# Layer 1's second product with its operands' roles exchanged: weight words stationary, blocks of 512 tokens moving

## The chip, the cores and the metric

One core of a Trainium2 chip runs the whole kernel. The metric is the device time of one execution in microseconds. The kernel before took 1139.12 us, the median of three runs (1136.8 to 1140.69).

## The reference

Chunked attention, then two feed-forward layers on the same 3072 tokens (4 batches of 768), all in float32; the weights are given in float64 on input.

```python
B, H, S, D = 4, 8, 768, 64          # attention: chunks of 32, 16 left, 8 right, 8 memory keys
scores = scale * q_c @ k_full.T     # per chunk; k_full = memory keys + the chunk's window
out_c = softmax(scores) @ v_full
x = out.transpose(0, 2, 1, 3).reshape(3072, 512)
h = x @ w_in                        # layer 1: 512 -> 2048
g = h * tanh(softplus(h))           # Mish
x = g @ w_out                       # 2048 -> 512: "layer 1's second product"
h = x @ w2_in                       # layer 2: 512 -> 2048
g = h * sigmoid(1.702 * h)
out = g @ w2_out                    # 2048 -> 512
```

## The kernel before, in words

The work runs in four stages that overlap at their seams: attention with layer 1's first product (`quads`, `forward`), layer 1's second product (`second(1, k)`), layer 2's first product (`first`), layer 2's second product (`second(2, k)`). Every matmul operand but the earliest is a pair of words, high and low (float32r): a high part is a rounded copy (ScalarE, or VectorE), a low part a VectorE difference, and a product is three matmuls: high-high, high-low, low-high.

**Order.** Every operation is given to a planner (`Plan`, lines 85 to 227) with a rank, a cost and the buffers that it reads and writes. The planner runs a list schedule: on each engine the ready operation of least rank. The order it finds is fixed in each engine's queue, and all DMAs but the earliest are issued from SP's queue in that order. `T[name].new` takes the next of a tag's buffers; it waits until the operations of the buffer's last use are done. One unit of rank in the second products is one product of 24 matmuls.

**Layer 1's first product** (`forward`, line 1004). For each block of 384 tokens (8 of them) and each of 16 slices of 128 features, 12 matmuls of 384 columns go to one of four PSUM banks; ScalarE or VectorE copies the bank to a staging buffer (gh and gl in turn, three buffers each), and SP stores it in DRAM as g1d. Features are on partitions, tokens in rows.

**Layer 1's second product** (`second`, line 1225). One level of Strassen-Winograd: tokens fall into two halves (th), features into two (fh), and outputs into two of 256 columns; instead of eight block products there are seven, on operands that are sums and differences of blocks (`comb`). A call `second(1, k)` takes 128 tokens of each half. It loads four blocks a11, a12, a21, a22 of 128 x 1024 numbers (8 feature slices of 128 tokens each) from g1d, applies Mish, and combines them. In `step` each operand is split into gh and gl, and 24 matmuls (8 slices x 3) go to one bank: the activations' words are the stationary operand (128 features x 128 tokens), the weights' words the moving one (256 columns). So the sums have tokens on partitions. `row` then turns them with four TensorE transposes of 128x128 against the identity, copies the bank of 512 columns to a u buffer and stores that in x1d, where features are on partitions again. There are 12 calls of 7 products.

**Layer 2's first product** (`first`, line 1161). Also seven products, here with weights stationary and 384 columns of x moving; `x_prep` (line 1073) loads x1d, forms differences in the v buffers, and splits the seven operands into homes named in `places` (line 1042). The first three operands are prepared during calls 9 and 10 of the second product (line 1387), the other four at its end.

Buffers that the change touches: `ql`, `kl`, `qT`, `kT`, `mem_t`, `aT` (attention), `gh`, `gl`, `u` (three buffers each), `mask`; and `own`, the four tiles wi0 to wi3 that layer 1's first weights leave free.

Of the kernel before, what the change touches and what calls it, by code (L numbers as in the profile page):

```python
# [27 lines left out]
class Buf:  # L28


    def __init__(self, tag, shape, dtype):
        self.tag, self.shape, self.dtype = tag, shape, dtype
        self.tile = None
        self.gate = []
        self.closed = False
        self.writers, self.readers, self.users = [], [], []
        self.whole = self

# [3 lines left out]
    def get(self):  # L42
        if self.tile is None:
# [12 lines left out]
class Tag:  # L56
# [4 lines left out]
    def new(self, shape, dtype):  # L61
        b = Buf(self, shape, dtype)
        self.made.append(b)
        return b
# [20 lines left out]
class Plan:  # L85
# [10 lines left out]
    def add(self, rank, ways, reads=(), writes=(), updates=(), chain=None, table=None):  # L96
# [33 lines left out]
        for b in (*reads, *writes, *updates):  # L130
            assert not b.whole.closed
            b.whole.users.append(op)
        if chain is not None:
# [109 lines left out]
def kernel(  # L243
# [46 lines left out]
    def tags(pool, **bufs):  # L290
# [214 lines left out]
    mask = fixed(sb.tile([P, 3, P], F32, name="mask"))  # L505
# [498 lines left out]
    def forward(j, f):  # L1004
# [31 lines left out]
        load(i + 0.4, gds[key], [lambda: (g1d[s, 2 * th + fh][:, p, :], t.get())], P * TB * 4, 1536, [t])  # L1036

    K2 = KD // 2
# [4 lines left out]
        ("ql", "kl", "qT", "kT"), ("gh", "gh", "gl", "aT"), ("gh", "aT", "gl", "gl"),  # L1043
# [29 lines left out]
    def x_prep(s, wanted, kts, rank, gap=0.0, stage="st", at="vt"):  # L1073
# [7 lines left out]
        def half(kt, a, rank):  # L1081
            if stage == "u" and kt and a:
                ts = [T[stage].new([P, TB], F32) for _ in range(2)]
                for i, t in enumerate(ts):
                    c = (2 * s + i) * TB
                    load(rank - 3, t, [lambda t=t, c=c: (t.get(), x1d[:, a * K2 + kt, c:c + TB])],
                         P * TB * 4, 1536, [x1s[3 * s + i] for i in range(3)])
                return [(t, t.get) for t in ts]
            st = T["st" if stage == "u" else stage].new([P, 2, TB], F32)
            load(rank - 3, st, [lambda: (  # L1090
                st.get(),
                x1d[:, a * K2 + kt, 2 * TB * s:2 * TB * (s + 1)].rearrange("p (s t) -> p s t", s=2),
            )], P * TB * 8, 3072, [x1s[3 * s + i] for i in range(3)])
# [129 lines left out]
    turn2 = [0]  # L1223

    def second(layer, k):
# [3 lines left out]
        r = RB[layer] + 7 * k  # L1229
        ha, hc = (T[x].new([P, H2], F32) for x in banks[k % 2])  # L1230
        src = (g1d, gd)[layer - 1]

        def block(blk, tag, rank):
            t = T[tag].new([P, NP, P], F32)
            load(rank - 2, t, [lambda: (t.get(), src[s, blk][:, :, j * P:(j + 1) * P])],
                 P * NP * P * 4, 512, [gds[layer, s, blk, p] for p in range(NP)])
            if layer == 1:
                add(rank, [("act", act(NP * P), lambda: nc.scalar.activation(
                    out=flat(t), in_=flat(t), func=AF.Mish))], updates=[t], table="mish")
# [9 lines left out]
        def step(i, n, src, bank, fresh):  # L1249
# [11 lines left out]
            w = [wb[layer, p, kind] for p in range(NP)]  # L1261
# [13 lines left out]
            if i == 0:  # L1275
                kw["writes"].append(pace.setdefault((layer, k), fixed()))
            add(r + i, [("pe", 3 * NP * 0.1175, go)], reads=reads, **kw)

        def row(th, t):
            r0 = 2 * TB * s + th * TB + j * P  # L1280
            if layer == 2:
                load(r + 6.5, fixed(), [lambda: (out[r0:r0 + P, :], t.get())], P * DM * 4, 2048, [t])
                return
# [157 lines left out]
```

## Time and profile before

| | |
|---|---|
| median of 3 runs (lowest, highest) | 1139.12 us (1136.8, 1140.69) |
| the profiled execution | 1139.0 us, span 1137.0 us |
| TensorE matmul / weight load busy | 98% / 94% |
| VectorE / ScalarE busy | 74% / 56% |
| granted TensorE clock, mean | 0.993 |
| DMA | 217.94 MB, mean 192 GB/s |

Busy is the union of an engine's recorded instructions. Matmuls are pipelined and their recorded durations overlap, so the pace of the engine is read from one start to the next. A group's name is out<-moving,stationary for a matmul, out<-in for others, without buffer numbers: o, s, h are PSUM banks; wo, wi, vt, xh, xl, u are buffers in SBUF. PE is TensorE's matmuls, PEld its weight loads, DVE VectorE, ACT ScalarE, SPq the queue that issues DMAs.

### The profile page before, as it was taken

How to read it: one execution, taken by the hardware profiler on the slowest of the kernel's cores; microseconds unless marked ns; L12 is line 12 of the kernel's file. 1: busy time of each engine (PE TensorE's matmuls, PEld its weight loads, DVE VectorE, ACT ScalarE, POOL GpSimd, SP SyncE). 2: the span in 40 equal slices, each digit the busy share in tenths (PEclk: the TensorE clock that was granted, in tenths of full speed). 3: DMA queues.
4: the chain of work that ended last, by engine and by line, in shares of the span. 5: the costliest groups of instructions: out<-in, count | busy, mean ns of one | idle time of the engine just before them, and what ended most of it. 6: DMA issues, size and time to landing. Idle time of an engine off the chain costs nothing.

```text
span 1137.0 us, 22649 instructions
## 1 busy us (share of the span) xinstructions
PE 1117.1 (98%) x8320; PEld 1070.3 (94%) x8320; DVE 841.8 (74%) x1878; ACT 632.3 (56%) x1478; POOL 10.1 (1%) x29
## 2 busy tenths in 40 slices
PE   7899999999999999999999999999999999999998
PEld 6667999999999999999999999999999999999998
DVE  5898877887776668779787776847566877786875
ACT  4776566666566456675675566555566443333422
POOL 2000000000000000000000000000000000000000
PEclk8899999999999999999999999999999999999999
DMA  9975778768976856556564478777688644536351
GB/s 167 276 205 140 205 203 249 200 166 219 233 231 223 259 152 196 169 156 201 174 187 137 129 255 257 247 249 240 227 262 266 200 133 122 148 103 166 112 151 53
DMA packets 325741, 217.94 MB, mean 192 GB/s; under 512 B 136120, under 2 KB 300743, under 8 KB 325631
## 3 DMA queue, kind: packets, MB, share of 16 engines
q1 hardware_dynamic: 325279, 215.76, 65.7%
q8 instruction: 65, 1.06, 0.4%
q0 software_dynamic: 352, 0.75, 0.4%
q14 instruction: 45, 0.37, 0.1%
HBM read 135.18 MB, written 81.26 MB: 190 GB/s over the span
## 4 chain that ended last, share of the span: by engine, by line
PE 93%; DVE 3%; DMA 1%; SPq 1%; ACT 1%; issue 0%; DVEq 0%; ACTq 0%
PE o L1268 18%; PE h L1019 13%; PE o L1019 13%; PE h L1268 12%; PE s L1268 11%; PE h L1179 9%; PE o L1179 8%; PE s L1179 4%; PE o L712 1%; PE s L712 1%; PE s L929 1%; PE o L929 1%; PE s L908 1%; PE o L908 1%; SPq L306 1%; PE o L1288 1%
## 5 line engine op out<-in xcount | busy, mean ns | idle before, releaser
L779 ACT ACTIVATE e<-e,mx 96x128 f32<-96x128 f32 x240 | 93.0, 394 | 4.8 <-DVE mx L764 4.8
L1268 PE MATMUL o<-wo,xh 128*128 128x256 f32 x456 | 85.8, 284 | 0.0
L1258 DVE TENSOR_TENSOR xl<-wi,xh 128x1024 fp32r<-128x1024 f32 x64 | 77.7, 1222 | 8.3 <-ACT xh L1255 7.4
L1019 PE MATMUL h<-xh,wi 128*128 128x384 f32 x320 | 83.8, 343 | 0.0
L1019 PE MATMUL o<-xh,wi 128*128 128x384 f32 x320 | 83.5, 342 | 0.0
L1258 DVE TENSOR_TENSOR xl<-vt,xh 128x1024 fp32r<-128x1024 f32 x48 | 58.3, 1222 | 20.1 <-ACT xh L1255 19.3
L1268 PEld LDWEIGHTS o<-wo,xh 128*128 128x128 f32 x456 | 70.6, 190 | 0.0
L1255 ACT ACTIVATE xh<-wi 128x1024 fp32r<-128x1024 f32 x50 | 52.6, 1054 | 23.1 <-PE h L1268 9.7
L1268 PE MATMUL o<-wo,xl 128*128 128x256 f32 x228 | 64.4, 283 | 0.0
L1268 PE MATMUL o<-wi,xh 128*128 128x256 f32 x312 | 58.7, 282 | 0.0
L1268 PE MATMUL s<-wo,xh 128*128 128x256 f32 x312 | 58.5, 283 | 0.0
L1019 PEld LDWEIGHTS h<-xh,wi 128*128 128x128 f32 x320 | 56.7, 188 | 1.7
L1019 PEld LDWEIGHTS o<-xh,wi 128*128 128x128 f32 x320 | 56.8, 188 | 1.3
L1019 PE MATMUL o<-xl,wi 128*128 128x384 f32 x160 | 53.8, 337 | 0.0
L1019 PE MATMUL h<-xl,wi 128*128 128x384 f32 x160 | 53.8, 336 | 0.0
L1149 ACT ACTIVATE e<-h 128x384 f32<-128x384 f32 (+1 forms) x53 | 23.5, 444 | 48.4 <-PE h L1268 35.0
L1268 PE MATMUL o<-wo,wi 128*128 128x256 f32 x342 | 48.3, 283 | 2.2 <-DVE wi L1258 1.5
L1268 PEld LDWEIGHTS s<-wo,xh 128*128 128x128 f32 x312 | 48.4, 190 | 0.0
L1268 PEld LDWEIGHTS o<-wi,xh 128*128 128x128 f32 x312 | 48.2, 190 | 0.0
L1268 PE MATMUL h<-wi,xh 128*128 128x256 f32 x256 | 47.5, 282 | 0.0
L1268 PE MATMUL h<-wo,xh 128*128 128x256 f32 x256 | 47.3, 281 | 0.0
L1268 PEld LDWEIGHTS o<-wo,wi 128*128 128x128 f32 x342 | 43.4, 188 | 3.3 <-DVE wi L1258 2.1
(404 smaller groups left out, 3185.8 us busy)
## 6 DMA issues: line engine op xcount, KB each, us to landing
st<-in_moe_w_out_dram SPq DMA_DIRECT2D x32, 512.0 KB
st<-wd SPq DMA_DIRECT2D x29, 512.0 KB
g1d<-gh SPq DMA_DIRECT2D x64, 192.0 KB
g1d<-gl SPq DMA_DIRECT2D x64, 192.0 KB
vt<-g1d SPq DMA_DIRECT2D x24, 512.0 KB
wi<-g1d SPq DMA_DIRECT2D x24, 512.0 KB
vt<-gd SPq DMA_DIRECT2D x24, 512.0 KB
wi<-gd SPq DMA_DIRECT2D x24, 512.0 KB
```

Source lines behind the costliest of these rows:

```text
L306: queue.dma_start(out=o, in_=i)
L712: nc.tensor.matmul(out=s[hh][:, keys(d, i, True), :], lhsT=queries(d, i), rhs=keys(d, i), start=True, stop=True)
L779: nc.scalar.activation(out=e[:, i, hh, :], in_=e[:, i, hh, :], func=AF.Exp, scale=-1.0, bias=mx[:, i, hh:hh + 1], accum_out=sm[:, first + ...
L908: nc.tensor.transpose(t[:, i, hh, :], e[:, i, hh, :], ident[:GQ, :GQ])
L929: nc.tensor.matmul(out=o[hh * D:(hh + 1) * D, g], lhsT=vt[g // per][:, g % per, h + hh], rhs=aTs[g // 2][:, g % 2, hh], start=True, stop=True,
L1019: nc.tensor.matmul(out=h.get(), lhsT=a[:, c], rhs=b.at(kk), start=(n == 0), stop=(n == KD * len(prods) - 1))
L1149: ("act", act(n, True), lambda: nc.scalar.activation(out=dst(), in_=bank.get(), func=AF.Copy)),
L1179: nc.tensor.matmul(out=bank.get(), lhsT=a, rhs=b, start=(fresh and m == 0), stop=(m == 3 * K2 - 1), skip_group_check=not fresh,)
L1255: ("act", act(NP * P), lambda: nc.scalar.activation(out=flat(gh), in_=flat(src), func=AF.Copy)),
L1258: add(rank + 0.05, [("dve", dve(NP * P), lambda: nc.vector.tensor_tensor(out=flat(gl), in0=flat(src), in1=flat(gh), op=ALU.subtract))], re ...
L1268: nc.tensor.matmul(out=bank.get(), lhsT=a[:, p], rhs=b, start=(fresh and p == 0 and m == 0), stop=(p == NP - 1 and m == 2), skip_group_che ...
L1288: nc.tensor.transpose(bank[:, m, :], t[:, m * P:(m + 1) * P], ident.get())
```

## The change

`second` keeps layer 2 alone; for layer 1 there is `across(k)`, six calls of 256 tokens of each half. In a half-product (h: four of eight feature slices) a weight word of 128x128 is the stationary operand and 256 tokens of gh or gl move; the two 128-wide parts of the outputs (d) go to the two halves of one bank. The sums have outputs on partitions and are stored in x1d as they are. Each block is two tiles of four slices x 256 tokens. For the first two calls a matmul into the h bank goes ahead of the first product, since a copy writes that bank before matmuls add to it. g1d and x1d get a layout in which a half's tokens follow one another.

z0 to z3 are four tiles of 1024 numbers a partition; in the attention stage `Shared` lays ql, kl, mem_t (z0), qT, kT (z1), gh (z2) and aT (z3) into them, two buffers for gh; gl and u have two buffers, and the mask becomes a buffer too. `places` gets other homes, and the first three x operands of layer 2 are prepared in the last six units of the stage, through wi2 and wi3.

```diff
     T = tags(
-        sb, st=2, v=2, xh=2, xl=2, gh=3, gl=3, u=3, ev=2,
-        ql=1, kl=1, qT=1, kT=1, vt=2, e=2, aT=2, mx=3, sm=3, r=3, mem_t=1,
+        sb, st=2, v=2, xh=2, xl=2, gl=2, u=2, w=1, ev=2,
+        z0=1, z1=1, z2=1, z3=1, vt=2, e=2, mx=3, sm=3, r=3, mask=1,
     )
+    z0, z1, z2, z3 = (T[x].new([P, 2 * DM], F32) for x in ("z0", "z1", "z2", "z3"))
+    T.update(ql=Shared(z0, 0), kl=Shared(z0, TB), mem_t=Shared(z0, TB + 32 * NKB), qT=Shared(z1, 0), kT=Shared(z1, 448))
+    T.update(gh=Shared(z2, 0, TB), aT=Shared(z3, 0, TB))
...
-    x1d = dram.tile([P, KD, NT], F32, name="x1d")
+    x1d = dram.tile([P, KD, 2, NS * TB], F32, name="x1d")
-    g1d = dram.tile([NS, 4, P, NP, TB], F32, name="g1d")
+    g1d = dram.tile([4, P, NP, NS * TB], F32, name="g1d")
...
     places = (
-        ("ql", "kl", "qT", "kT"), ("gh", "gh", "gl", "aT"), ("gh", "aT", "gl", "gl"),
+        ("gl", "gl", "mask", "w"), ("z0", "z1"), ("z2", "z3"),
         ("xh",), ("xl",), own[0:2], own[2:4], ("xh",), ("xl",),
     )
...
+    def across(k):
+        r = L1 + 14 * k
+        x0, n2 = k * W2, HP * W2
+        ha, hc = (T[x].new([P, 2, W2], F32) for x in banks[k % 2])
...
+        def block(blk, names, rank):
+            ts = [T[x].new([P, HP, W2], F32) for x in names]
+            for h, t in enumerate(ts):
+                load(rank + h - 4, t, [lambda h=h, t=t: (
+                    t.get(), g1d[blk][:, HP * h:HP * (h + 1), x0:x0 + W2]
+                )], P * n2 * 4, 1024, [gds[1, s, blk, HP * h + p] for s in around for p in range(HP)])
+                add(rank + h, [("act", act(n2), lambda t=t: nc.scalar.activation(
+                    out=flat(t), in_=flat(t), func=AF.Mish))], updates=[t], table="mish")
+            return ts
...
+        def step(i, n, srcs, bank, fresh):
+            kind, half = BT[n]
+            for h, src in enumerate(srcs):
+                names = (("xh", "xl"), own[0:2], ("xh", "xl"))[turn1[0] % 3]
...
+                prime = [hb] if k < 2 and i == h == 0 else []
+
+                def go(h=h, gh=gh, gl=gl, w=w, prime=prime):
+                    for b in prime:
+                        nc.tensor.matmul(
+                            out=b.get().rearrange("p d c -> p (d c)"), lhsT=w[0][0][:, :P],
+                            rhs=gh[:, :2].rearrange("p a c -> p (a c)"), start=True, stop=True,
+                        )
+                    for d in range(2):
+                        for p, (t, c, _) in enumerate(w):
+                            c += half * H2 + d * P
+                            wh, wl = t[:, c:c + P], t[:, DM + c:DM + c + P]
+                            for m, (a, b) in enumerate(((wh, gh), (wl, gh), (wh, gl))):
+                                nc.tensor.matmul(
+                                    out=bank[:, d, :], lhsT=a, rhs=b[:, p, :],
...
+        def keep(rank, th, dh, t):
+            load(rank, x1s.setdefault(k, fixed()), [lambda: (
+                x1d[:, K2 * dh:K2 * (dh + 1), th, x0:x0 + W2], t.get()
+            )], P * DM * 4, 1024, [t])
...
+        c11, p4, p5, u2 = (T[x].new([P, 2, W2], F32) for x in ("u", "ev", "e", "e"))
+        a11 = block(0, ("z0", "z1"), r - 5)
+        a22 = block(3, own[2:4], r - 2.6)
+        a12 = block(1, ("vt", "vt"), r - 0.6)
+        a21 = block(2, ("z2", "z3"), r + 0.6)
+        hd = T["o3"].new([P, 2, W2], F32)
+        hb = T["h"].new([P, 2, W2], F32)
+        step(0, 0, a11, ha, True)
+        copy(r + 1.1, View(hb), ha, DM)
+        step(1, 5, a22, hd, True)
+        copy(r + 3.2, View(p4), hd, DM)
+        step(2, 2, a12, ha, False)
+        copy(r + 5.1, View(c11), ha, DM)
+        keep(r + 5.2, 0, 0, c11)
+        comb(r + 1.6, a22, a21, a22, ALU.add)
+        comb(r + 2.1, a21, a11, a21, ALU.subtract)
+        step(3, 4, a22, hc, True)
+        copy(r + 7.1, View(p5), hc, DM)
+        comb(r + 3.2, a11, a22, a11, ALU.subtract)
+        step(4, 1, a11, hb, False)
+        copy(r + 9.1, View(u2), hb, DM)
+        comb(r + 5.4, a12, a12, a11, ALU.subtract)
+        step(5, 6, a12, hc, False)
+        plus(r + 11.1, u2, hc)
+        keep(r + 11.2, 0, 1, u2)
+        step(6, 3, a21, hb, False)
+        plus(r + 13.05, p5, hb)
+        plus(r + 13.06, p4, hb)
+        keep(r + 13.2, 1, 1, p5)
+        keep(r + 13.2, 1, 0, p4)
...
-        def row(th, t):
...
-            bank = T["o2"].new([P, KD, P], F32)
-
-            def turn():
-                for m in range(KD):
-                    nc.tensor.transpose(bank[:, m, :], t[:, m * P:(m + 1) * P], ident.get())
-
-            x = T["u"].new([P, KD, P], F32)
-            rank = r + (7.4, 6.4)[th]
-            add(rank, [("pe", 0.45, turn)], reads=[t, ident], writes=[bank])
-            copy(rank + 0.1, View(x), bank, DM)
...
-    WB = {1: (0, 6), 3: (0, 7), 5: (1, 6), 7: (1, 7)}
-    for k1 in range(3 * NS):
-        second(1, k1)
-        if k1 in WB:
-            part, p = WB[k1]
-            w_words(2, part, p, RB[1] + 7 * k1 + 6, [pace[1, k1]], ("v", "v"))
-        if k1 in (9, 10):
-            x_prep(0, ORD[:3], [k1 - 9], RB[1] + 7 * k1 + 4, 0, "st", "v")
+    for k1, (part, p) in enumerate(((0, 6), (0, 7), (1, 6), (1, 7), (None, 0), (None, 0))):
+        across(k1)
+        if part is not None:
+            w_words(2, part, p, RB[1] + 14 * k1 + 13, [pace[1, k1]], ("v", "v"))
+    x_prep(0, ORD[:3], range(2), RA - 6, 1.5, own[2:4], "v")
     w_in2(0, RA - 4)
```

## Rows read from the trace of the kernel before

**Rows 1.** The page's first part: busy us (share of span) xinstructions.

```profile
span 1137.0 us, 22649 instructions
PE 1117.1 (98%) x8320; PEld 1070.3 (94%) x8320; DVE 841.8 (74%) x1878; ACT 632.3 (56%) x1478; POOL 10.1 (1%) x29
```

**Rows 2.** The page's chain of work that ended last, by engine.

```profile
PE 93%; DVE 3%; DMA 1%; SPq 1%; ACT 1%; issue 0%; DVEq 0%; ACTq 0%
```

**Rows 3.** Busy time in stretches: PE, PEld, DVE, ACT, POOL, clock, DMA share, GB/s.

```profile
100.00:400.00 300.00, 300.00 (x2257) 282.92 (x2256) 225.59 (x832) 178.22 (x616) 3.09 (x12) 1.00 0.77 215
401.00:640.00 239.00, 237.98 (x2006) 237.53 (x2005) 189.32 (x227) 155.87 (x207) 0.00 (x0) 1.00 0.55 167
640.00:660.00 20.00, 19.51 (x147) 18.99 (x146) 16.61 (x30) 10.22 (x19) 0.00 (x0) 1.00 0.60 190
...
885.00:900.00 15.00, 13.81 (x102) 13.29 (x101) 14.09 (x19) 7.44 (x14) 0.00 (x0) 1.00 0.68 208
```

**Rows 4.** Timeline of TensorE, two products of layer 1's second: start, us, what.

```profile
401.28 0.41 PE L1268 MATMUL s<-wo,xh 128*128 128x256 f32 x2
...
404.16 1.58 PE L1268 MATMUL o<-wo,wi 128*128 128x256 f32 x12
405.57 1.59 PE L1268 MATMUL o<-wi,wi 128*128 128x256 f32 x12
407.00 0.41 PE L1268 MATMUL s<-wo,xh 128*128 128x256 f32 x2
```

**Rows 5.** Timeline of TensorE, end of layer 2's first product.

```profile
886.33 1.20 PE L1179 MATMUL o<-xh,wi 128*128 128x384 f32 x6
887.37 1.20 PE L1179 MATMUL h<-xl,wi 128*128 128x384 f32 x6
888.41 0.40 PE L1268 MATMUL s<-wo,xh 128*128 128x256 f32 x2
```

**Rows 6.** The transposes' line: count, ns min/median/max, first and last start us.

```profile
L1288 PE MATMUL o<-ident,ev x48: 271/272/273, 424.1 to 654.4; 128*128 128x128 f32 x48
...
L1288 PE MATMUL o<-ident,u x48: 270/272/273, 427.4 to 657.0; 128*128 128x128 f32 x48
```

**Rows 7.** Timeline of TensorE about one group of four transposes.

```profile
424.12 0.60 PE L1288 MATMUL o<-ident,ev 128*128 128x128 f32 x4
424.47 0.49 PE L1268 MATMUL o<-wo,xh 128*128 128x256 f32 x2
424.79 0.29 PE L1268 MATMUL o<-wo,xl 128*128 128x256 f32 x1
424.92 0.40 PE L1268 MATMUL o<-wo,xh 128*128 128x256 f32 x2
425.15 0.28 PE L1268 MATMUL o<-wo,xl 128*128 128x256 f32 x1
425.27 0.40 PE L1268 MATMUL o<-wo,xh 128*128 128x256 f32 x2
```

**Rows 8.** ScalarE's copies from banks o to u, 401 to 658 us.

```profile
L1149 ACT ACTIVATE u<-o x29: 383/597/610, 425.1 to 657.3; 128x512 f32<-128x512 f32 x23, 128x256 f32<-128x256 f32 x6
```

**Rows 9.** Timelines of ScalarE and SP: copies to gl, a store.

```profile
276.34 0.49 ACT L1149 ACTIVATE gl<-h 128x384 f32<-128x384 f32 x1 [0.52 <-PE h L1019]
...
285.57 0.42 SPq L306 DMA_DIRECT2D g1d<-gl  x1
...
287.67 0.49 ACT L1149 ACTIVATE gl<-h 128x384 f32<-128x384 f32 x1 [3.63 <-PE h L1019]
```

**Rows 10.** Timeline about a change of group in layer 2's first product.

```profile
709.02 0.92 SPq L306 DMA_DIRECT2D u<-x1d  x2
...
711.25 0.50 ACT L1196 ACTIVATE u<-o 128x384 f32<-128x384 f32 x1 [0.55 <-PE o L1179]
...
717.67 0.55 DVE L1104 TENSOR_TENSOR vt<-u,vt 128x384 f32<-128x384 f32 x1
```

**Rows 11.** VectorE's x differences (L1104) and low parts (L1118), 560 to 640 us.

```profile
L1104 DVE TENSOR_TENSOR v<-st x2: 548/550/551, 577.0 to 584.5; 128x384 f32<-128x384 f32 x2
...
L1118 DVE TENSOR_TENSOR gl<-v,aT x1: 553/553/553, 594.8 to 594.8; 128x384 fp32r<-128x384 f32 x1
```

**Rows 12.** The DMA view: the slowest recorded landing, KB each, us to landing.

```profile
wi<-in_q_dram POOLq DMA_DIRECT2D x1, 192.0 KB, 8.6
```

More of the change, by code (lines that the diff above doesn't have):

```diff
@@ L37, in __init__ @@
         self.whole = self
+        self.inside = None
     def __getitem__(self, key):
@@ L42, in get @@
     def get(self):
+        if self.tile is None and self.inside is not None:
+            dims = self.shape[1:]
+            n = 1
+            for d in dims:
+                n *= d
+            names = "abc"[:len(dims)]
+            self.tile = self.inside.get()[:, self.at:self.at + n].rearrange(
+                f"p ({' '.join(names)}) -> p {' '.join(names)}", **dict(zip(names, dims))
+            )
         if self.tile is None:
@@ L62, in new, with __init__ @@
         b = Buf(self, shape, dtype)
+        self.made.append(b)
+        return b
+class Shared:
+    def __init__(self, whole, *at):
+        self.inside, self.places, self.bufs = whole, at, len(at)
+        self.made = []
+    def new(self, shape, dtype):
+        b = Buf(self, shape, dtype)
+        b.inside, b.at = self.inside, self.places[len(self.made) % self.bufs]
         self.made.append(b)
@@ L132, in add @@
             b.whole.users.append(op)
+            if b.whole.inside is not None:
+                assert not b.whole.inside.closed
+                b.whole.inside.users.append(op)
         if chain is not None:
@@ L504 @@
     ident = fixed(sb.tile([P, P], F32, name="ident"))
-    mask = fixed(sb.tile([P, 3, P], F32, name="mask"))
+    mask = T["mask"].new([P, 3, P], F32)
     def mask_of(g):
@@ L1035, in forward @@
         gds[key] = fixed()
-        load(i + 0.4, gds[key], [lambda: (g1d[s, 2 * th + fh][:, p, :], t.get())], P * TB * 4, 1536, [t])
-    K2 = KD // 2
+        load(i + 0.4, gds[key], [lambda: (g1d[2 * th + fh][:, p, s * TB:(s + 1) * TB], t.get())], P * TB * 4, 1536, [t])
+    K2, HP, W2 = KD // 2, NP // 2, 2 * P
     ORD = (0, 4, 1, 2, 6, 3, 5)
@@ L1081, in half @@
         def half(kt, a, rank):
+            after = [x1s[k] for k in range(s * TB // W2, ((s + 1) * TB - 1) // W2 + 1)]
+            src = x1d[:, a * K2 + kt, :, TB * s:TB * (s + 1)]
             if stage == "u" and kt and a:
@@ L1084, in half @@
                 for i, t in enumerate(ts):
-                    c = (2 * s + i) * TB
-                    load(rank - 3, t, [lambda t=t, c=c: (t.get(), x1d[:, a * K2 + kt, c:c + TB])],
-                         P * TB * 4, 1536, [x1s[3 * s + i] for i in range(3)])
+                    load(rank - 3, t, [lambda t=t, i=i: (t.get(), src[:, i, :])], P * TB * 4, 1536, after)
                 return [(t, t.get) for t in ts]
[L1089 to L1093, printed above, removed]
+            name = "st" if stage == "u" else stage if isinstance(stage, str) else stage[a]
+            st = T[name].new([P, 2, TB], F32)
+            load(rank - 3, st, [lambda: (st.get(), src)], P * TB * 8, 1536, after)
             return [(st, lambda i=i: st[:, i]) for i in range(2)]
@@ L1228, in second @@
+    def second(k):
         s, j = divmod(k, 3)
-        r = RB[layer] + 7 * k
+        r = RB[2] + 7 * k
         ha, hc = (T[x].new([P, H2], F32) for x in banks[k % 2])
-        src = (g1d, gd)[layer - 1]
         def block(blk, tag, rank):
             t = T[tag].new([P, NP, P], F32)
[L1235 to L1239, printed above, removed]
+            load(rank - 2, t, [lambda: (t.get(), gd[s, blk][:, :, j * P:(j + 1) * P])],
+                 P * NP * P * 4, 512, [gds[2, s, blk, p] for p in range(NP)])
@@ L1260, in step @@
             kind, half = BT[n]
-            w = [wb[layer, p, kind] for p in range(NP)]
+            w = [wb[2, p, kind] for p in range(NP)]
             def go():
@@ L1407 @@
     for k2 in range(3 * NS):
-        second(2, k2)
+        second(k2)
     with tc.manual_schedule():
```

54 lines of the change are left out of this document (37 added, 17 removed).

## The prediction

> **What bounds the kernel now.** I read the page's head first: TensorE is busy for 1117.1 of a span of 1137.0 us, VectorE 842, ScalarE 632 [rows 1]; busy shares alone don't prove a bound, so the chain of waits came next, and 93% of it is TensorE [rows 2]. Then the stretches. In the attention and first-product stage (100 to 400 us) TensorE is busy for all of 300 us, in layer 1's second product (401 to 640) for 237.98 of 239, over the passage into layer 2 (640 to 660) for 19.51 of 20, at a granted clock of 1.00, which is the upper level, 2.4 GHz [rows 3]. VectorE has 50 us to spare in the second product and ScalarE 83. So what leaves TensorE's stream there leaves the span, and what leaves the other engines is worth nothing, unless they turn late.
>
> The profiled execution took 1139.0 us with a span of 1137.0, so 2.0 us lie around the span; the three runs have a median of 1139.12, 0.1 us from it. I add to 1139.0. A measurement of this kernel tells about 0.3% from no change: 3.4 us, so faster is below 1135.7 and slower above 1142.5.
>
> **The change part by part.**
>
> *Matmuls of the product.* Before: 12 blocks x 7 products x 24 matmuls of 256 columns = 2016. After: 6 blocks x 14 half-products x 24 = 2016, again 256 columns. Only the roles change: weights stand still, activations move. Two products of before take 401.28 to 407.00, 5.72 us for 48, or 119.2 ns each [rows 4]; 256 columns at 2.4 GHz are 106.7, so 12.5 ns go with each. Layer 2's first product already has weights stationary: 12 matmuls of 384 columns in 2.08 us, 173.3 ns, 13.3 over the 160.0 of its columns [rows 5]. If that surplus belongs to the orientation, the change costs 2016 x 0.8 ns = 1.7 us; if it belongs to the width, nothing. Before, two of three consecutive matmuls share a stationary operand, afterwards none do, yet before, too, every matmul has a weight load of its own, 8320 of each [rows 1]. I take +1.0, between -1.7 and +1.7.
>
> *Row transposes.* They go: 48 + 48 = 96 [rows 6], 24 groups of four. What a group costs is read from starts, not durations: from its first transpose at 424.12 to 424.92 lie four transposes and three matmuls, 0.80 us; three matmuls are 3 x 0.119 = 0.36. So 0.44 us, and 24 x 0.44 = 10.6 us [rows 7]. TensorE was busy through all of these stretches, so I put the whole on the path: -10.6, between -8.5 (0.355 a group, from 424.12 to 424.47, should the slow matmul behind it have another cause) and -10.8 (0.45 a group).
>
> In a sentence apart: the Trainium skill, "TensorE: Matmul & The Clock Gate", Part 4 (PE-mode transpose), prices a 128x128 transpose at about 275 ns inside a kernel; the rows have 272 ns as the duration, but starts 89 ns apart. By the page's figure the term would be an estimated 96 x 0.275 = 26.4 us instead of 10.6 (a rival below).
>
> *Evacuation of the transposes.* The 24 copies of 512 columns go with them, 0.597 us each on ScalarE [rows 8], 14.3 us. Products' sums are copied in pieces of 512 columns instead of 256, half as many. Mish (48 of 1024 columns), operand splits (84 high, 84 low) and block combinations (48) stay equal in number and size. ScalarE and VectorE have the slack above: 0. Without it, should TensorE have waited for them, the gain would be part of the next term.
>
> *Waits inside the stage.* TensorE idles 1.02 us in 401 to 640 [rows 3]. A bank's copy now has two half-products behind which to finish, 48 matmuls or 5.7 us, where it had one product of 2.9. The one-buffer operand pairs z0/z1, wi2/wi3, z2/z3 are free again 4 to 10 half-products (11 to 29 us) before their next use. I take -1.0; bounds -1.0 and +2.0 (the idle time twice over).
>
> *The two priming matmuls* of 512 columns: 384 columns take 173.3 ns and 256 take 119.2, so a column costs 0.42 ns and each of these about 0.23: +0.5.
>
> *DMAs.* The stage's 48 loads of g1d and 24 stores of x1d stay at 512 and 256 KB, in pieces twice as long; the engines' share there is 0.55 [rows 3], so I take 0. If bandwidth there were short it would show as ScalarE waiting for g1d, which is off the path today.
>
> *Fewer staging buffers in the attention stage.* gh and gl fall from three buffers to two each, u as well. A copy into gl now waits for the store of the copy two before it. In a crowded place one gl copy runs at 276.34, the second after it at 287.67, and the store of the first is issued only at 285.57 [rows 9]: from its issue's end to the later copy 1.7 us remain. The store then waits in the SP queue, the copy waits in ScalarE's order, and behind it exponentials of the next attention block, which TensorE needs. Cover: ScalarE has 122 of 300 us free, and a bank waits for four first products. In layer 2's first product the second u load was issued at 709.0, before g0 at 711.25, and used at 717.7 [rows 10]. With two buffers it follows that g0's store, and some 3 us are left for the load, with the next group's ready products (1.04 us each [rows 5]) as filler. I take +0.5 for both; bounds 0 and +3 (the three changes of group at 1 us each).
>
> *The passage from layer 1 to layer 2.* The first three x operands, prepared before about 595 us today (first difference at 577, last low part at 595), move to the last 6 half-products. Their four differences and six low parts take VectorE 10 x 0.55 = 5.5 us [rows 11], beside six activations on ScalarE. In 640 to 660 VectorE is busy for 16.61 of 20 [rows 3]; 3.4 are free, so 2.1 do not fit. Their four loads wait for wi2/wi3, on SP, and behind them there stand the weight loads for layer 2 and the last stores. The third operand's home, z2/z3, is free only when the last half-product's operands have been split; until then its difference sits in one of the two v buffers and holds the second pair up. TensorE has the two ready products of the group as filler. Today's passage costs 0.49 us, and the other passage (885 to 900) 1.19 [rows 3]. I take +1.5; bounds 0 and +5.5 (all of the moved work on the path).
>
> Sum: -10.6 + 1.0 - 1.0 + 0.5 + 0.5 + 1.5 = -8.1, so 1139.0 - 8.1 = **1130.9 us**. What is late next is still TensorE's own stream; at the passage, VectorE.
>
> **The rivals.**
>
> *The gain is eaten by the attention stage.* For it: if each 20 us has one place like that of [rows 9], there are 15 in 100 to 400; the order on ScalarE is fixed, and a held copy holds what follows. If each of them holds TensorE for 0.5 us, that is 7.5 instead of 0.5: 1130.9 + 7.0 = 1137.9, no change. Against it: TensorE has not one idle microsecond in 100 to 400, and the copies of [rows 9] were held up by TensorE, not by a store.
>
> *The passage becomes serial, slower than before.* Mechanism: both rounds of x loads go through the one pair wi2/wi3, and the second round starts only after the v buffer is free, that is behind the last operands. Price: the longest landing that the trace records for a load, 8.6 us for 192 KB, at the crowded start [rows 12], twice: 17.2 instead of 1.5, so 1146.6. It decides from 13.1 us of standstill. For it: the single pair, the two v buffers, z2/z3. Against it: wi2/wi3 are last read by the fourth product, 6 half-products or 17 us before the end, and the DMA engines' share is 0.60 there.
>
> *The transposes were worth their durations.* If TensorE's stream waited for each transpose's 272 ns, the term would be 96 x 0.272 = 26.1 and the time 1139.0 - 26.1 + 2.5 = 1115.4. Against it: the starts in [rows 7].
>
> *Orientation and passage at their upper ends*: 1130.9 + 0.7 + 4.0 = 1135.6, at the edge of what can be told from no change; it is the top of the forecast's own range.
>
> **How the numbers follow.** The forecast with its bounds (1127.5 to 1135.6): 0.79. Eaten: 0.11. Serial passage: 0.07. Durations: 0.03. Faster by over 0.3% takes in the forecast and the durations, 0.82; within 0.3%: 0.11; slower: 0.07. Lower end 1127.5: all but the transposes and the priming at their best, 1139.0 - 10.6 + 0.5 - 1.7 - 1.0 = 1126.2, raised by 1.3 since not all are likely at once. The upper end takes in half of the eaten case: 1137.
>
> **What would show it.** Transposes: line 1288's rows gone, and the stretch from the first across matmul to layer 2's first one about 10 us shorter, with 256-column starts still 119 ns apart; 117 or 121 would mean that the orientation counts. Waits inside: TensorE idle under 1 us in the stage. Staging: gh or gl copies that wait for a store of g1d, and TensorE under 300 of 300 us before 400. Passage: a gap of 1 to 2 us before layer 2's first products, ended by VectorE or ScalarE. The prediction is wrong if the stage is shortened by 10 us and the span is not, or if TensorE idles over 5 us at the passage.

## The result and the profile after

The changed kernel takes 1125.34 us, the median of four runs (1124.0 to 1128.12); the kernel before took 1138.85 beside it, and the ratio is 0.9885 [0.9859, 0.9911]. So it is faster, by 13.5 us where the forecast had 8.1, and 1125.34 lies below the range of 1127.5 to 1137.0.

Two profiles of the changed kernel are used: the first took 1128.12 us, the highest of its runs, the second, of the same code, 1125.69, close to the median. Head and chain of the first, which answer to [rows 1, 2]:

```profile
span 1126.0 us, 22455 instructions
PE 1107.1 (98%) x8226; PEld 1063.5 (94%) x8226; DVE 847.8 (75%) x1868; ACT 602.9 (54%) x1398; POOL 14.7 (1%) x35
...
PE 92%; DMA 3%; DVE 2%; ACT 1%; SPq 1%; issue 1%; DVEq 0%; ACTq 0%
```

8320 + 2 - 96 = 8226 matmuls: the transposes are gone, the two priming ones are there. Stretches of the second profile (columns as in [rows 3]):

```profile
100.00:400.00 300.00, 300.00 (x2272) 285.64 (x2271) 223.47 (x827) 177.53 (x601) 7.83 (x18) 1.00 0.80 223
400.00:640.00 240.00, 240.00 (x2010) 239.96 (x2009) 207.28 (x236) 132.14 (x153) 0.00 (x0) 1.00 0.53 167
640.00:660.00 20.00, 19.98 (x119) 19.59 (x119) 14.26 (x30) 14.61 (x30) 0.00 (x0) 1.00 0.84 271
```

TensorE stands nowhere from 100 to 640, and for 0.02 us in the 20 us of the passage. Its timeline at the start of the second product (start, us, what), to set beside [rows 4]:

```profile
398.72 0.39 PE L1299 MATMUL h<-xh,wo 128*128 128x512 f32 x1
398.95 0.40 PE L1308 MATMUL s<-xh,wo 128*128 128x256 f32 x2
...
401.77 3.04 PE L1308 MATMUL s<-wi,wo 128*128 128x256 f32 x24
404.64 0.40 PE L1308 MATMUL o<-xh,wo 128*128 128x256 f32 x2
```

24 matmuls from 401.77 to 404.64: 119.6 ns each; over all 2016 the mean from one start to the next is 119.1. The priming matmul holds the stream for 0.23 us (398.72 to 398.95).

Where the 13.4 us between the two spans (1137.0 and 1123.6) lie. Each matmul is charged the time from its own start to the next matmul's start, idle time included, and these are summed by line. The second product begins with its first priming matmul, which is counted in the row of its own.

| us | before | after | change | forecast |
|---|---|---|---|---|
| start of the span to the first matmul of layer 1's first product | 41.53 | 41.00 | -0.53 | 0 |
| from there to the second product | 359.75 | 357.72 | -2.03 | +0.5 |
| row transposes | 8.51 | 0 | -8.51 | } -10.6 |
| the second product's 2016 matmuls | 242.94 | 240.20 | -2.74 | } +1.0 -1.0 |
| priming, two | 0 | 0.46 | +0.46 | +0.5 |
| layer 2's first product (the passage is in it) | 237.32 | 237.54 | +0.22 | +1.5 |
| layer 2's second product | 242.62 | 242.36 | -0.26 | 0 |
| last matmul's start to the end of the span | 4.31 | 4.32 | +0.01 | 0 |

The surplus lies in the stage ahead of the change, and in costs that did not come.

### The profile page after: what moved, and what is told of

The parts are those of the page before. It is cut to its first block, busy times and chain, and to the rows that moved or that the text cites. A ratio compares the mean times of both kernels' runs of the same rounds, so it can differ in the third digit from the quotient of the medians.

```text
span 1126.0 us, 22455 instructions
## 1 busy us (share of the span) xinstructions
PE 1107.1 (98%) x8226; PEld 1063.5 (94%) x8226; DVE 847.8 (75%) x1868; ACT 602.9 (54%) x1398; POOL 14.7 (1%) x35
## 4 chain that ended last, share of the span: by engine, by line
PE 92%; DMA 3%; DVE 2%; ACT 1%; SPq 1%; issue 1%; DVEq 0%; ACTq 0%
PE h L1049 13%; PE o L1049 13%; PE o L1400 9%; PE o L1308 9%; PE h L1207 8%; PE h L1400 6%; PE s L1308 6%; PE o L1207 6%; PE s L1400 6%; PE h L1308 6%; PE s L1207 4%; PE o L742 1%; DMA st<-wd 1%; PE s L742 1%; PE o L959 1%; PE s L959 1%
## 5 line engine op out<-in xcount | busy, mean ns | idle before, releaser
L809 ACT ACTIVATION_READ_ACCUMULATOR e<-e,mx 96x1 f32 x240 | 46.0, 192 | 0.0
L1400 PE MATMUL o<-wo,xh 128*128 128x256 f32 x232 | 43.8, 282 | 0.0
L1390 DVE TENSOR_TENSOR xl<-wi,xh 128x1024 fp32r<-128x1024 f32 x32 | 38.9, 1222 | 3.5 <-ACT xh L1387 2.7
L1308 PE MATMUL o<-xh,wo 128*128 128x256 f32 x224 | 40.5, 282 | 0.0
L1390 DVE TENSOR_TENSOR xl<-vt,xh 128x1024 fp32r<-128x1024 f32 x24 | 29.3, 1222 | 13.5 <-ACT xh L1387 12.8
L1291 DVE TENSOR_TENSOR xl<-z,xh 128x1024 fp32r<-128x1024 f32 x24 | 29.3, 1224 | 11.9 <-ACT xh L1287 10.8
L1049 PE MATMUL h<-wo,wi 128*128 128x384 f32 x192 | 36.7, 340 | 0.0
L1400 PEld LDWEIGHTS o<-wo,xh 128*128 128x128 f32 x232 | 35.8, 190 | 0.0
L1049 PE MATMUL o<-wo,wi 128*128 128x384 f32 x192 | 35.2, 337 | 0.0
L1308 PEld LDWEIGHTS o<-xh,wo 128*128 128x128 f32 x224 | 34.7, 191 | 0.0
L1049 PEld LDWEIGHTS h<-wo,wi 128*128 128x128 f32 x192 | 33.2, 188 | 0.7
```

Source lines behind the costliest of these rows:

```text
L809: nc.scalar.activation(out=e[:, i, hh, :], in_=e[:, i, hh, :], func=AF.Exp, scale=-1.0, bias=mx[:, i, hh:hh + 1], accum_out=sm[:, first + ...
L1049: nc.tensor.matmul(out=h.get(), lhsT=a[:, c], rhs=b.at(kk), start=(n == 0), stop=(n == KD * len(prods) - 1))
L1291: add(rank + 0.05, [("dve", dve(n2), lambda gh=gh, gl=gl, src=src: nc.vector.tensor_tensor(out=flat(gl), in0=flat(src), in1=flat(gh), op=A ...
L1308: nc.tensor.matmul(out=bank[:, d, :], lhsT=a, rhs=b[:, p, :], start=(fresh and h == d == p == m == 0), stop=(h == 1 and p == HP - 1 and m ...
L1390: add(rank + 0.05, [("dve", dve(NP * P), lambda: nc.vector.tensor_tensor(out=flat(gl), in0=flat(src), in1=flat(gh), op=ALU.subtract))], re ...
L1400: nc.tensor.matmul(out=bank.get(), lhsT=a[:, p], rhs=b, start=(fresh and p == 0 and m == 0), stop=(p == NP - 1 and m == 2), skip_group_che ...
```

## The experiments

Each was timed in five rounds beside the kernel before, which took 1139.2 to 1139.8 us there.

**The changed kernel again**, unedited, as the base for the others.

> The changed kernel once more, for its spread against the kernel before on one chip, with the granted clock of every run. Theory A (the transposes, and fewer switches of TensorE between full products and attention's small matmuls): about 12.5 us below the kernel before at equal clock (10.6 transposes, 2 switches, 0.7 waits inside the stage, less 0.5 for priming, rest even), near 1126. Theory B (the part beyond the forecast is the clock: more half-rate windows fell into the runs of before): at equal granted clock only 8 to 9 us lie between the two.

1125.98 us (1124.05 to 1126.82), ratio 0.9885 [0.9866, 0.9903]. The size stands; it is no accident of the first runs, and theory B falls: the granted clock of these runs was 0.992 to 0.995, that of the kernel before beside them 0.992 to 0.997.

**Transposes put back** into the changed kernel: 24 groups of four into a free bank, read by nobody.

```diff
+        turned_bank = T["o2"].new([P, KD, P], F32)
...
+                    for m in range(4 * ((2 * i + h) in (3, 6, 10, 13))):
+                        nc.tensor.transpose(turned_bank[:, m, :], ident.get(), ident.get())
                     for d in range(2):
...
```

> The changed kernel with 24 groups of four transposes of the identity put back among the half-products, into a free bank that nobody reads: weights stationary as changed. Theory A: 10.6 us above the changed kernel, 0.44 a group. Theory C: 8.5, or less if weights-stationary products take the switch without a slow first matmul. If a transpose cost its duration: 26.

1136.67 us, ratio 0.9975 [0.9963, 0.9987]: 10.7 over the changed kernel, or 0.445 a group. The timeline has the pattern of [rows 7]. Four transposes take 0.36 us, and the first of the matmuls behind them holds the stream for 0.202 us instead of 0.119 (mean of the 24 groups):

```profile
424.76 0.60 PE L1305 MATMUL o<-ident 128*128 128x128 f32 x4
425.12 1.67 PE L1311 MATMUL s<-wi,wo 128*128 128x256 f32 x12
```

TensorE, VectorE and ScalarE run all their other operations in the order of the changed kernel, so nothing but the transposes differs. The term's size is right, in this kernel. Whether it was also the price in the kernel before is the next question.

**Transposes taken out of the kernel before**, first by storing the row tiles as they are, then by copying each tile to the u buffer, so that its own buffer comes free as before (the diff is that of the second).

```diff
-            bank = T["o2"].new([P, KD, P], F32)
-            def turn():
-                for m in range(KD):
-                    nc.tensor.transpose(bank[:, m, :], t[:, m * P:(m + 1) * P], ident.get())
-            x = T["u"].new([P, KD, P], F32)
+            x = T["u"].new([P, DM], F32)
...
-            add(rank, [("pe", 0.45, turn)], reads=[t, ident], writes=[bank])
-            copy(rank + 0.1, View(x), bank, DM)
+            copy(rank + 0.1, View(x), t, DM)
...
```

> The kernel before without its 96 transposes and the 24 copies behind them; the sums are stored in x1d as they lie, tokens on partitions, so layer 2 computes on wrongly ordered numbers: the turning is left out. Attention stage and orientation as before. Theory A: 10.6 us below the kernel before, 0.44 us for each of 24 groups. Theory C: 8.5 (the four starts alone), the rest of the change's gain being the orientation's.

> The kernel before without its 96 row transposes, but with everything else of their path: the row tile is copied SBUF to SBUF into a u buffer and the u buffer is stored, so tiles are held no longer than before. The turning is left out, so the output is not the reference's. Theory A (the transposes and the slow matmul behind each group, 24 x 0.44 us, are TensorE's own time on the path, and the kernel that stored the tiles unturned stood still because its stores held the tiles): 1139.2 - 10.5 = 1128.7 us, starts in the second product 119 ns apart with no stalls. Rival B (without the transposes another chain, VectorE's splits and combinations and weight words, is as long as a call of seven products, so TensorE waits for low parts as in that run): 1138 to 1143 us, with about 1 us of standstill in most of the 12 calls. Between: 1132 to 1136, half of the gain eaten.

1142.69 us, ratio 1.0037 [1.0024, 1.0049], and 1141.48, ratio 1.0018 [1.0009, 1.0026]. Neither is faster: both theories of the first run miss, and rival B of the second holds. With the copies, the product's line takes 251.2 us; before, with the transposes' line, it took 242.9 + 8.5 = 251.4. What left TensorE's stream came back, 8.1 us of it as standstill (240 less 231.86 in the first row below). Layer 2's first product takes 4.0 us more than before: 1.9 are more standstill, and 1.7 go with the clock, granted at 0.66 from 660 to 665 behind a standstill of 1.14 us. The stretches with the copies, the waits of TensorE from 400 to 660 (who <- whom, us, times, longest) and one such place:

```profile
400.00:640.00 240.00, 231.86 (x1923) 229.38 (x1922) 190.69 (x231) 152.31 (x204) 0.00 (x0) 1.00 0.56 167
640.00:660.00 20.00, 17.95 (x131) 17.06 (x131) 16.22 (x30) 9.11 (x16) 0.00 (x0) 1.00 0.55 172
```

```profile
PE s L1268 <- DVE xl L1258: 2.8, 3, 1.3
PE h L1268 <- DVE wi L1258: 2.1, 2, 1.2
PE h L1268 <- DVE xl L1258: 1.2, 1, 1.2
```

```profile
473.36 0.39 PE L1268 MATMUL h<-wo,wi 128*128 128x256 f32 x2
474.71 1.45 PE L1268 MATMUL h<-wo,wi 128*128 128x256 f32 x10 [0.95 <-DVE wi L1258]
```

TensorE stands about 1 us at a time for VectorE's low parts (L1258), though VectorE is busy for only 191 of 240. Under TensorE's full stream lay something else that takes as long, which the profile of before could not show, since nothing waited for it. It need not be a limit of the buffers or of the data: the planner wrote a new order here, in which about 50 of VectorE's 255 operations from 401 to 660 stand elsewhere than before, and no run takes the transposes out with the order kept.

**Which limit?** Theory: the operand blocks' buffers. The layout-alone kernel (below) with the four blocks in z0 to z3 in every other of the first nine calls and loads two units earlier, without and with transposes (without them the copies go to a u and an e buffer in turn, with them to u alone):

```diff
-            t = T[tag].new([P, NP, P], F32)
-            load(rank - 2, t, ...
+            if layer == 1 and k < 9 and k % 2:
+                t = T["z%d" % blk].new([P, NP, P], F32)
+            else:
+                t = T[tag].new([P, NP, P], F32)
+            load(rank - 4, t, ...
```

> The layout-alone kernel (the changed kernel's buffers, but layer 1's second product as before) without its 96 row transposes: the row tile is copied SBUF to SBUF and stored unturned, so the output is not the reference's; and in every other call of the first nine, the four blocks a11, a12, a21, a22 go to the free tiles z0 to z3 and are loaded two units earlier, so that a block's buffer is not waited for. Theory A (in the kernel before, a loop as long as a call of seven products lies behind TensorE's stream, and it runs through the operand buffers: release, 5 us of load, Mish, split, combinations): with the buffers doubled, the standstill of about 1 us a call goes from calls 0 to 8 and about three quarters of 10.5 us come through: 1139.5 - 8 = 1131.5 us. Rival B (the loop is VectorE's own order, buffers or not): 1139 to 1142 us, with about 1 us of standstill in most calls.

> The same doubled block buffers and earlier loads, but with the 96 row transposes in place as before. Theory A: with the transposes TensorE sets the pace of every call, so room behind it is worth nothing but the two or three stalls that are there, 0 to 1.5 us: 1138 to 1140 us, and the difference to the kernel without the transposes is about 8 us. Rival B (the loop is VectorE's own order): also 1138 to 1140, and no difference to the kernel without the transposes.

Without transposes 1136.49 us, ratio 0.998 [0.9968, 0.9993]; with them 1138.32, ratio 0.9991 [0.9981, 1.0001]. The difference is 1.8 us, not 8. Inside the stage 5.1 us come through: the product's line takes 246.6 us without transposes, and 243.2 + 8.5 = 251.7 with them. But layer 2's first product then takes 242.3 instead of 238.5. It waits for its operands at the passage (1.2 us of it in one place for an x split on ScalarE), 1.3 us longer in all than with transposes, and 1.7 us more go with the clock, granted at 0.69 from 660 to 665 behind that wait:

```profile
400.00:640.00 240.00, 235.10 (x1944) 232.93 (x1943) 198.95 (x247) 145.40 (x193) 0.00 (x0) 1.00 0.53 160
640.00:660.00 20.00, 17.36 (x114) 15.78 (x113) 15.79 (x34) 9.66 (x19) 0.00 (x0) 0.99 0.76 251
```

So the seam is one limit. That the buffers are another is likely, not shown: the line is 4.5 us shorter than in the run with the copies above, but that kernel had the old layout too, and no run has the new layout without transposes and without the room. What the rest is was not separated. A candidate, argued from these rows only, is VectorE's fixed order: the sums `plus` (L1297 before, L1322 after) wait for the product's end, and the next low parts are queued behind them. VectorE's waits for them, before (401 to 640) and after (400 to 640):

```profile
DVE u L1297 <- PE s L1268: 14.6, 6, 3.9
DVE ev L1297 <- PE h L1268: 9.0, 9, 2.4
DVE u L1297 <- PE o L1268: 8.6, 5, 3.3
```

```profile
DVE e L1322 <- PE o L1308: 3.4, 3, 2.7
DVE e L1322 <- PE h L1308: 1.5, 2, 0.9
DVE e L1322 <- PE s L1308: 1.3, 2, 0.7
```

32.2 us before, 6.2 after.

**Layout alone**: the changed kernel's buffers, homes and DRAM layouts, with the second product, its transposes and the early x operands of before (`across(k)` replaced by `second1(k)`, the old `second` for layer 1).

> The new buffers, homes and layouts of g1d and x1d, but layer 1's second product as before: tokens stationary, 12 calls, 96 transposes, first x operands prepared early. Theory A: the order that the planner finds for the attention stage has 47 entries from full products into small matmuls instead of 64, each worth 0.1 to 0.2 us, so 1.5 to 3 us below the kernel before, and the second product starts about 2 us earlier. Theory C (turning the product round is what gained more than its transposes: weights stationary run at a better pace): no difference from the kernel before, within 0.7 us. My forecast had +0.5 for this part.

1139.89 us, ratio 1.0009 [0.9997, 1.0022]: no gain. Yet up to the second product its trace has the whole gain of the changed kernel: 357.54 us from the first full matmul, where before took 359.75. It is lost later: the product's line takes 244.3 (242.9 before), layer 2's two products 238.4 and 243.7 (237.3 and 242.6), 3.6 us in all. So the gain ahead of the second product is the layout's, and the changed kernel keeps it. Why the layout alone doesn't was not separated.

**What the layout changes in the attention stage.** TensorE has no idle time there before or after, so I counted its order. From the 193rd full matmul of layer 1's first product (384 columns) to the second product, both kernels run 1280 full matmuls and 864 small ones of the attention. Before, TensorE goes from a full product into small ones 60 times and takes 286.28 us; after, 43 times and 284.17 (the expectations count the priming matmul with it: 284.40, and a gain of 1.88 for 16 entries); the layout alone has the very order of after, and 284.17. Other runs with one of these two orders agree within 0.02 us. One visit to the scores (L712) and one to the turns (L908, transposes of 96 rows) in the kernel before, then a change from scores to turns in the changed one:

```profile
202.40 0.51 PE L1019 MATMUL o<-xh,wi 128*128 128x384 f32 x2
202.75 0.34 PE L1019 MATMUL o<-xl,wi 128*128 128x384 f32 x1
203.02 1.12 PE L712 MATMUL o<-kT,qT 64*96 64x128 f32 x16
204.07 0.62 PE L1019 MATMUL h<-xh,wi 128*128 128x384 f32 x2
204.53 0.34 PE L1019 MATMUL h<-xl,wi 128*128 128x384 f32 x1
...
206.11 0.34 PE L1019 MATMUL h<-xl,wi 128*128 128x384 f32 x1
206.28 0.82 PE L908 MATMUL s<-ident,e 96*128 96x96 f32 x8
206.89 0.59 PE L1019 MATMUL h<-xh,wi 128*128 128x384 f32 x2
207.31 0.34 PE L1019 MATMUL h<-xl,wi 128*128 128x384 f32 x1
```

```profile
214.86 1.12 PE L742 MATMUL s<-z 64*96 64x128 f32 x16
215.91 0.30 PE L938 MATMUL o<-ident,e 96*128 96x96 f32 x1
```

The last full matmul ahead of the scores holds the stream for 0.27 us (202.75 to 203.02) instead of 0.174, the first one behind them for some 0.28 (two take 0.46). Values (the products with the values, whose stationary operand is 64 wide) cost the same. Ahead of turns a full matmul takes 0.17 (206.11 to 206.28), so entering them costs nothing; behind them it takes 0.26. Sixteen scores take 1.05 us whether a full product follows or another small group, but eight turns take 0.61 us between full products, 0.66 behind scores and 0.75 ahead of scores. So a visit that is merged with another saves up to 0.2 us, and 2.11 / 17 = 0.12 on the mean. To test it, the planner's choice for TensorE was changed, after a small operation to prefer a full product ("apart", 82 visits in the whole stage instead of 48 by the planner's own count):

```diff
+                    if e == "pe" and not op.full and now > 100 and run < 1:
+                        if held is None:
+                            held = item
+                        else:
+                            kept.append(item)
+                        continue
...
+                if e == "pe":
+                    run = run + 1 if op.full else 0
```

> The changed kernel with the opposite rule in the planner, from 100 us of its own time on: after a small operation (scores, turn, values) no second small one is placed while a full product is ready. TensorE then enters small operations from full products 82 times instead of 48; work and buffers are the same, and full products are used up no sooner. Theory A (0.1175 us an entry): 34 x 0.1175 = 4.0 us more, 1130.0 us against 1126.0; the stretch from the 193rd full matmul to the second product takes 288.4 us instead of 284.40, without idle time. Rival B (entries are a by-product, the 1.88 us came from the buffers): 284.4 and 1126. Rival C (small operations come late and TensorE waits): idle time of TensorE in 100 to 400 us and more than 4 us lost.

1143.02 us, ratio 1.0028 [1.0013, 1.0043], 17 over the changed kernel: theory A's 4 us, and rival C on top. Its stretches:

```profile
100.00:400.00 300.00, 291.14 (x2173) 271.80 (x2172) 227.70 (x835) 167.53 (x572) 6.54 (x15) 0.98 0.76 212
400.00:640.00 240.00, 240.00 (x1971) 239.90 (x1970) 200.55 (x225) 126.60 (x147) 0.00 (x0) 1.00 0.52 168
```

The stretch from the 193rd full matmul to the priming matmul takes 303.04 us. 8.86 of them are idle, and about 5 go with the clock (0.98 over 300 us: some 10 us at the lower level, half of them lost); the other 289.2 are 5.0 more than 284.17, for 33 more visits, but also for 20 small matmuls that fall into this stretch here. The price can be read without that subtraction, from starts alone, at the upper level and where no wait lies between: what the last full matmul ahead of a visit and the first behind it take beyond 0.174 us is 0.155 us a visit in the order with 60 visits, 0.151 in that with 43 and 0.142 in that with 76; 9.4, 6.5 and 10.6 us in all. Between the first two that is 2.8 us. Small groups give back 1.1, the turns ahead of scores above all, and the other full matmuls take 0.4 ns less each, 0.4 us in all, for which no run shows a reason. So the visits, not the buffers as such, carry most of the 2.11 us. Which of the layout's changes made the planner write the order with fewer visits was not separated.

**Fewer visits**, in three runs: small operations are held until 2 full products ran (in the kernel before), until 3 (in the changed one), and until 4, for the first five attention blocks alone (`op.rank < 72`). The condition is all that differs from the edit above:

```diff
+                    if e == "pe" and not op.full and 0 < run < HOLD:
...
```

> The kernel before, with one rule added to the planner's list schedule for TensorE: after a full product has been placed, small operations (scores, turns, values of the attention, and the row transposes) are held until 2 full products ran, unless nothing else is ready. In the attention stage TensorE's stream then enters small operations from full products 41 times instead of 64; amount of work and buffers are those of before. Theory A (what the changed kernel gained ahead of the second product came from fewer such entries: 64 to 48 gave about 2.0 us, 0.125 us each): 23 entries fewer give 2.9 us, the second product starts about 357 us after the first-product stage's first matmul instead of 359.75, and the time is 1136.3 us against 1139.2. Rival B (the gain came from the changed buffers, the entries are a by-product): the second product starts at 359.75 within 0.3, time 1139. Rival C (held operations come late and TensorE waits): idle time in 100 to 400 us, time above 1140.

> The changed kernel with the same rule in the planner, held until 3 full products ran: 35 entries from full products into small operations instead of 48. Theory A (0.125 us an entry): 13 x 0.125 = 1.6 us, 1124.4 us against 1126.0, and the second product starts about 356.3 us after the first matmul of the first-product stage instead of 357.95. Rival B (entries are a by-product): 1126. Rival C (held operations come late): TensorE idle in 100 to 400 us, 1127 or more.

> The changed kernel with the planner's hold rule limited to attention operations of rank under 72 (the first five of eight attention blocks), held until 4 full products ran: 34 entries from full products into small operations instead of 48, and the last three blocks planned as they were. In the run with the unlimited rule the stock of full products was used up at the last block, TensorE stood for 6.4 us behind its scores' exponentials, and its clock was at the lower level for some 8 us behind that. Theory A (0.1175 us an entry, from 16 entries and 1.88 us): 14 x 0.1175 = 1.6 us, 1124.4 us against 1126.0, and the stretch from the 193rd full matmul to the second product takes 282.8 us instead of 284.40. Rival B (entries are a by-product): 284.4 and 1126. Rival C (the last blocks still come late, the stock is used up): a standstill before 400 us, 1128 or more.

1150.99 us, ratio 1.0103 [1.008, 1.0126]; 1135.83, 0.9961 [0.9946, 0.9976]; 1146.2, 1.0061 [1.0049, 1.0073]. All three miss, by rival C. Waits of TensorE in the three kernels, the longest group of each:

```profile
PE o L924 <- DVE e L815: 4.2, 1, 4.2
```

```profile
PE o L954 <- DVE e L845: 6.4, 1, 6.4
```

```profile
PE s L758 <- DVE r L768: 6.8, 2, 3.4
```

Held scores reach VectorE and ScalarE late, the full products are used up, and TensorE stands for a turn or a score. Their times say nothing on the price of a visit; they show that neither order had time to spare in the attention's own chain.

**Later x operands**: the first three operands of layer 2 prepared 4 half-products later.

```diff
-    x_prep(0, ORD[:3], range(2), RA - 6, 1.5, own[2:4], "v")
+    x_prep(0, ORD[:3], range(2), RA - 2, 1.5, own[2:4], "v")
```

> The changed kernel with the first three x operands of layer 2 prepared 4 half-products (11.4 us) later in rank, so that their loads, differences and splits are planned in the last two units instead of the last six. If the passage of the changed kernel was nearly free only because the preparation fitted in front of it (theory A: the 20 us ahead have room for it), the stall appears now: 2 to 6 us of TensorE idle about 635 to 650 us, 1128 to 1132 us. Rival B (the products that are ready at the passage, with the prepared operands' order set by data alone, cover it anyway): within 0.5 us of the changed kernel, 1126.

1125.94 us, ratio 0.9878 [0.9861, 0.9894], against 1125.98: rival B. The passage in its trace, with 0.57 us idle (layer 2's first product takes 238.9 there instead of 237.5, a loss too small to show in the time), and how the changed kernel (second profile) crosses it:

```profile
640.00:660.00 20.00, 19.43 (x107) 18.08 (x106) 16.54 (x33) 12.99 (x27) 0.00 (x0) 1.00 0.87 260
```

```profile
630.84 0.52 PE L1207 MATMUL s<-gl,wo 128*128 128x384 f32 x2
...
637.61 1.21 PE L1207 MATMUL s<-z,wo 128*128 128x384 f32 x6
...
641.48 1.21 PE L1207 MATMUL h<-z,wo 128*128 128x384 f32 x6
```

Layer 2's first two groups of matmuls, at 630.84 and 637.61, stand between the last half-products, 11 us ahead of the seam at 641.48. TensorE has one of two stages to go on with, and the preparation can move by 11 us without a loss that the time shows.

## Why the prediction was wrong

The direction, the cause of the larger part and its size were right. The sum was 5.4 us short: three terms of cost did not come as forecast, and one of them was a gain. That one alone put the time outside the range, for with +0.5 in its place 1125.34 would be 1127.9. The best cases that the prediction added up gave 1126.2, still above what was measured, as none of them had this term below nothing.

- *Transposes, -10.6*: 8.5 us on their own line and 24 slow matmuls behind them, 84 ns late each, 2.0: 10.5. Putting them back cost 10.7. The reason given, that TensorE was busy throughout and so the whole is on the path, was not enough: in the kernel before, planned anew without them, their removal alone gave nothing. The term came out because in the new stage nothing else takes their place (TensorE is busy for 240.00 of 240), which the prediction did not weigh. That much was luck.
- *Orientation, +1.0*: +0.3. Without the waits and the slow matmuls, 256 columns take 119.0 ns with activations stationary over the whole stage (119.2 in [rows 4]) and 119.1 with weights stationary. The surplus goes with the width, as the second of the two readings had it.
- *Waits inside, -1.0*: as forecast, 1.02 us idle before and 0.00 after. With the slow matmuls' -2.0 and the +0.3 this is the line's -2.7.
- *Priming +0.5, DMAs and copies 0*: as forecast; 0.23 us for each priming matmul.
- *Fewer staging buffers, +0.5*: **the step that failed.** It measured -2.0, 2.5 off and of the other sign. The step asked what two buffers instead of three would make wait, and took the order of the work as given. But the planner writes that order, and with the new buffers and layouts it wrote one with 17 visits fewer. [rows 3] with 300.00 busy of 300 seemed to leave nothing to win there; the visits' 0.1 us at either end lie inside the busy time. That the new order was the better one was luck too: nothing in the change aimed at it.
- *Passage, +1.5*: about 0 (+0.2 over the whole of layer 2's first product), 0.02 us idle in 640 to 660. The 5.5 us of VectorE's work were set against the 3.4 free in the last 20 us of before; in the changed kernel they lie ahead, between the last operand splits from 630 on, and VectorE is busy for only 14.26 of the 20 us of the passage.
- *The start*: -0.5, not forecast. It can't be put down to the change: the first full matmul starts at 38.3 to 42.6 us over these profiles, with a granted clock up to there of 0.955 in the earliest and 0.865 in the latest.

Of the rivals, none came: no standstill in the attention stage, none at the passage, and a transpose is worth its start distance of 89 ns and a quarter of the delay behind its group, not its 272 ns. The Trainium skill, "TensorE: Matmul & The Clock Gate", Part 4 (PE-mode transpose), with about 275 ns for 128x128 in bf16, is near the duration; the 10.7 us of 96 transposes show that the time on the path is 111 ns each.

## What to carry to other kernels

A bound engine's busy time says that nothing else is slower, not by how much: before counting work taken from it as a gain, look for what is next (buffers' release, load and preparation; sums that wait in an engine's order ahead of the next operands), or take the work out alone and see. Work put back into a fixed order is the cleaner test, since taking it out can change the order too. Where an order is planned from buffers and costs, a change of buffers can change the order elsewhere: compare the order itself, and count its changes between kinds of matmul. Two stages that can alternate at a seam can hide its preparation, as here.

## What was not expected of the hardware

A change from full float32r matmuls to the attention's scores or values and back costs some 0.1 us at either end, inside the busy time (rows above). To turns it costs nothing, back from them 0.08. Between scores and values it costs nothing that can be seen, from turns to scores 0.15.

After a standstill of 6.41 us, which ended at 367.8, the clock was granted at 0.51 from 370 to 375, that is nearly always at the lower level, 1.2 GHz (the run held until 3 products, stretches as in [rows 3]):

```profile
360.00:370.00 10.00, 3.02 (x18) 2.43 (x18) 8.11 (x18) 7.46 (x19) 0.00 (x0) 0.73 1.03 361
370.00:375.00 5.00, 5.00 (x28) 4.78 (x29) 2.17 (x5) 0.49 (x1) 0.00 (x0) 0.51 0.47 146
```

In the first profile of the changed kernel two waits of 0.78 and 1.04 us at 880 to 882 stood beside a clock of 0.84 and 0.82 (rows below). In the second they took 0.43 and 0.76 us, and the clock stayed at 1.00. Layer 2's second product took 1.6 us longer in the first, a part of the 2.4 us between the two profiles:

```profile
880.00:885.00 5.00, 3.34 (x19) 3.14 (x20) 5.00 (x6) 2.63 (x4) 0.00 (x0) 0.84 0.56 204
885.00:890.00 5.00, 5.00 (x37) 5.00 (x37) 3.33 (x6) 0.94 (x3) 0.00 (x0) 0.82 0.01 3
```

So a standstill at a seam can cost more than its own length.
